# Delaying two stages of a row-tile loop by one tile: the GELU sigmoid and the layernorm backward of a gated-MLP block

## The chip, the cores and the metric

The kernel runs on one core of a Trainium2 chip. The metric is device time in microseconds of one execution. The kernel before takes 1046.89 us (median of 6 runs, 1042.96 to 1053.63); its profiled execution took 1043.44 us, with a span of 1041.7 us from the first to the last instruction.

A core has five engines with instruction streams of their own: PE (matrix multiply, with its weight loads shown as PEld), DVE (vector), ACT (scalar functions), POOL and SP. Each stream is worked through in order. Matrix products land in PSUM, which has 8 banks of 512 float32 values per partition; ACT or DVE bring them from there to SBUF. Transfers to and from HBM are issued by SP, ACT or POOL.

## What is computed

The reference is forward and backward of two pre-layernorm blocks on x of 2048 rows (S) by 512 columns (D), in bfloat16: a linear attention block, then a gated MLP whose gate mixes the rows. Outputs are the result and the gradients of x and of six weights. Cut to what the change touches:

```python
def _B_ref(x, w_in, w_sp, b_sp, w_out):        # F = 1376, Fh = 688
    z = gelu_tanh(x @ w_in)                    # S x F
    z1 = z[..., :Fh]
    z2 = layernorm(z[..., Fh:])
    g = w_sp @ z2 + b_sp                       # mixes rows: S x S times S x Fh
    return (z1 * g) @ w_out

h = x + A(layernorm(x))
out = h + B(layernorm(h))
# and the vjp of out with respect to x and the weights, for a given grad_out
```

The kernel writes tanh-GELU as z * sigmoid(1.5958 * (z + 0.0447 z^3)). Its derivative needs z and the sigmoid s again: dz = (s + z * s * (1 - s) * (a + 3ab z^2)) * dgelu. So forward stores z (tensor `XZ`) and s (tensor `SG`) in HBM and backward loads them.

## The kernel before

It is written in a language whose framework orders each engine's instructions itself: the program gives the operations and the buffer pools, and the framework places the instructions of each engine by their dependences and its own estimates of time, and adds the waits. A pool with `bufs=2` gives two copies of each tile of it; a tile name that is asked for again takes the older copy and waits until all its users are done. There are 16 row tiles (NT) of 128 rows (P), DC = 4 column chunks of D, and 11 chunks of F (the last of 96).

Forward: `hnF` is the normalised h, transposed. The loads of `WspT` are transposing transfers issued from SP.

```python
# psZ: 2 buffers of 3 PSUM banks; xm, sgm: 4 buffers; x2, wt: 2 buffers
for m in range(NT):
    dma_T(WspT[:, m, :], B_w_sp[:, m * P:(m + 1) * P])
...
for m in range(NT):
    psz = psZ.tile(...)
    mm(psz, hnF chunk m, Win)                                        # 12 matmuls
    xm = p2r.tile([P, F], BF16, name="xm")
    nc.scalar.activation(xm[:], psz[:, 0:F], AF.Copy)                # line 474
    dma(XZ_v[:, m, 0:F], xm[:], nc.gpsimd)
    x2 = p2q.tile(...)
    nc.vector.tensor_tensor(out=x2[:], in0=xm[:], in1=xm[:], op=ALU.mult)        # 478
    nc.vector.tensor_scalar(x2[:], x2[:], b_c, 1.0, op0=ALU.mult, op1=ALU.add)   # 480
    wt = p2q.tile(...)
    nc.vector.tensor_tensor(out=wt[:], in0=x2[:], in1=xm[:], op=ALU.mult)        # 483
    sg = p2r.tile([P, F], BF16, name="sgm")
    nc.scalar.activation(sg[:], wt[:], AF.Sigmoid, scale=a_c)        # line 486
    dma(SG_v[:, m, 0:F], sg[:], nc.scalar)
    nc.vector.tensor_tensor(out=zT[:, m, :], in0=xm[:], in1=sg[:], op=ALU.mult)  # 489
ln_stats_all(p2s, lambda m: zT[:, m, Fh:F], ...)                     # bn_stats, line 213
for m in range(NT):
    # normalise zT[:, m, Fh:F] in place                              # line 494
...
for t in range(NT):                                                  # g: 16 x 32 matmuls
    mm(psg, WspT[:, m, t-th chunk], zT[:, m, Fh:])                   # over all m
```

Backward, the stage with the second loop. `pssp` holds 2 banks, `psW` 3, `ps3bt` 2 and `psH` 1: eight in all.

```python
for t in range(NT):                       # gradient of w_sp (out_5), 2 x 12 matmuls per t
    ... psw5 -> w5 (ACT) -> out_5

NJ1 = min(3, DC)
psw0 = psW.tile([P, NJ1, 512], F32, name="psw4")
for m in range(NT):
    # load sm (SG), xm2 (XZ), dzm (DZG)
    # dZT[:, m, :] = (s + z s (1 - s) (a + 3ab z^2)) * dzm    six DVE operations, one on ACT
    for j in range(NJ1):                                             # line 737
        nc.tensor.matmul(psw0[:, j, :], hnT2[:, m, j-th chunk], dZT[:, m, 0:512], ...)
    # 11 transposes of dZT[:, m] into pstZ (line 741), evicted to dzf by ACT
    psd = psH.tile([P, 512], F32, name="psdh")
    mm(psd[:, :], dzf, WinT)                                         # 11 matmuls
    # doutm <- grad_out
    ln_bwd(psd, hnT2[:, m], ..., dhT[:, m, :], resid=doutm)          # lines 223 to 241

# w_in gradient (out_4): jobs (j, gi), 4 column chunks x 3 groups of F, NJ1 jobs per pass
with tc.tile_pool(name="p3bo", bufs=2) as p3bo:
    for pi, job in enumerate([first] + passes):
        if pi > 0:
            psw0 = psW.tile([P, NJ1, 512], F32, name="psw4")         # one buffer
            # 16 x NJ1 matmuls                                       # line 767
        for slot, (j, gi) in enumerate(job):
            w4 = p3bo.tile([P, 512], BF16, name="w4")
            evac_copy(w4, psw0[:, slot])
            dma(out_4[...], w4)
```

After it `oT2` is loaded and `dhT` transposed (line 813) into `dhF`, both where this stage's tiles had lain; 64 matmuls of `oT2` with `dhT` follow (`psw4o`, line 819), and a loop that multiplies `dhF` with `WoT`, copies it on ACT (line 831) and works on it on DVE (lines 834 to 841).

Of the kernel before, what the change touches and what calls it, by code (L numbers as in the profile page):

```python
# [8 lines left out]
BF16 = mybir.dt.bfloat16  # L9
# [4 lines left out]
P = 128  # L14
# [13 lines left out]
def kernel(  # L28
# [74 lines left out]
    def note(eng, ns):  # L103
        busy[eng] += ns
# [354 lines left out]
    with tc.tile_pool(name="p2w", bufs=1) as p2w, \  # L459
            tc.tile_pool(name="p2s", bufs=6) as p2s, \  # L460
            tc.tile_pool(name="psZ", bufs=2, space=bass.MemoryType.PSUM) as psZ, \
            tc.tile_pool(name="ps2t", bufs=1, space=bass.MemoryType.PSUM) as ps2t:
        WspT = p2w.tile([P, NT, S], BF16, name="WspT")
        for m in range(NT):
            dma_T(WspT[:, m, :], B_w_sp[:, m * P:(m + 1) * P])

        with tc.tile_pool(name="p2r", bufs=4) as p2r, tc.tile_pool(name="p2q", bufs=2) as p2q:
            for m in range(NT):
                psz = psZ.tile([P, max(F, D)], F32, name="psZ")
                for (gs, gw) in F_grp:  # L470
                    mm(psz[:, gs:gs + gw],
                       [(hnF[:, j, m * P:(m + 1) * P], Win[:, j, gs:gs + gw]) for j in range(DC)])
                xm = p2r.tile([P, F], BF16, name="xm")
                nc.scalar.activation(xm[:], psz[:, 0:F], AF.Copy)  # L474
                note("act", (172 + F) / 1.2)
                dma(XZ_v[:, m, 0:F], xm[:], nc.gpsimd)
                x2 = p2q.tile([P, F], BF16, name="x2")
                nc.vector.tensor_tensor(out=x2[:], in0=xm[:], in1=xm[:], op=ALU.mult)
                note("dve", (58 + F / 2) / 0.96)
                nc.vector.tensor_scalar(x2[:], x2[:], b_c, 1.0, op0=ALU.mult, op1=ALU.add)  # L480
                note("dve", (58 + F / 4) / 0.96)
                wt = p2q.tile([P, F], BF16, name="wt")
                nc.vector.tensor_tensor(out=wt[:], in0=x2[:], in1=xm[:], op=ALU.mult)
                note("dve", (58 + F / 2) / 0.96)
                sg = p2r.tile([P, F], BF16, name="sgm")
                nc.scalar.activation(sg[:], wt[:], AF.Sigmoid, scale=a_c)  # L486
                note("act", (222 + F) / 1.2)
                dma(SG_v[:, m, 0:F], sg[:], nc.scalar)
                nc.vector.tensor_tensor(out=zT[:, m, :], in0=xm[:], in1=sg[:], op=ALU.mult)
                note("dve", (58 + F / 2) / 0.96)  # L490
        p2R_stack.close()
        ln_stats_all(p2s, lambda m: zT[:, m, Fh:F], Fh, mean3[:], rstd3[:], "3")
        for m in range(NT):
            nc.vector.tensor_scalar(zT[:, m, Fh:F], zT[:, m, Fh:F], mean3[:, m:m + 1], rstd3[:, m:m + 1],  # L494
                                    op0=ALU.subtract, op1=ALU.mult)
            note("dve", (58 + Fh / 4) / 0.96)
        if "zg" in dbg:
            dma(dbg["zg"].rearrange("(m p) f -> p m f", p=P), zT[:], nc.sync)

        gR = gR_stack.enter_context(tc.tile_pool(name="gR", bufs=1, side="right"))  # L500
        GT = gR.tile([P, NT, Fh], BF16, name="GT")
        pre3 = pre3_stack.enter_context(tc.tile_pool(name="pre3", bufs=1, side="right"))
        Wout_n = pre3.tile([P, NFHC, D], BF16, name="Wout_n")
        for k, (ks, kw) in enumerate(Fh_ch):
            dma(Wout_n[:kw, k, :], B_w_out[ks:ks + kw, :], nc.scalar)
        doutT = pre3.tile([P, NT, D], BF16, name="doutT")
        dma(doutT[:], G_v, nc.gpsimd)

        for t in range(NT):
            psg = psZ.tile([P, max(F, D)], F32, name="psZ")  # L510
            for (gs, gw) in Fh_grp:
                mm(psg[:, gs:gs + gw],
                   [(WspT[:, m, t * P:(t + 1) * P], zT[:, m, Fh + gs:Fh + gs + gw]) for m in range(NT)])
            nc.scalar.activation(GT[:, t, :], psg[:, 0:Fh], AF.Identity, bias=bspT[:, t:t + 1])  # L514
            note("act", (172 + Fh) / 1.2)
        if "G" in dbg:
            dma(dbg["G"].rearrange("(m p) f -> p m f", p=P), GT[:], nc.sync)
        uR = uR_stack.enter_context(tc.tile_pool(name="uR", bufs=1, side="right"))
        UT = uR.tile([P, NT, Fh], BF16, name="UT")
        nc.vector.tensor_tensor(out=UT[:], in0=zT[:, :, 0:Fh], in1=GT[:], op=ALU.mult)  # L520
        note("dve", (58 + NT * Fh / 2) / 0.96)
# [138 lines left out]
    with tc.tile_pool(name="p3b", bufs=1) as p3b, \  # L660
# [1 line left out]
            tc.tile_pool(name="pssp", bufs=1, space=bass.MemoryType.PSUM) as pssp, \  # L662
            tc.tile_pool(name="psW", bufs=1, space=bass.MemoryType.PSUM) as psW, \
            tc.tile_pool(name="ps3bt", bufs=1, space=bass.MemoryType.PSUM) as ps3bt, \
            tc.tile_pool(name="psH", bufs=1, space=bass.MemoryType.PSUM) as psH:
        WinT = p3b.tile([P, NFC, D], BF16, name="WinT")
        for k in range(NFF):
            dma_T(WinT[:, k, :], B_w_in[:, k * P:(k + 1) * P])
# [19 lines left out]
        with tc.tile_pool(name="p3sp", bufs=2) as p3sp:  # L688
# [15 lines left out]
                    dma(out_5[t * P:(t + 1) * P, rs0:rs0 + width], w5[:].rearrange("p a b -> p (a b)")[:, 0:width],  # L704
                        nc.sync if t % 2 == 0 else nc.gpsimd)

            NJ1 = min(3, DC)
            cg0s, cg0w = F_grp[0]
            psw0 = psW.tile([P, NJ1, 512], F32, name="psw4")
            with tc.tile_pool(name="p3bg", bufs=2) as p3bg, \  # L710
                    tc.tile_pool(name="p3bd", bufs=2) as p3bd:
                for m in range(NT):
                    sm = p3bg.tile([P, F], BF16, name="sm")
                    dma(sm[:], SG_v[:, m, 0:F], nc.scalar)
                    xm = p3bg.tile([P, F], BF16, name="xm2")
                    dma(xm[:], XZ_v[:, m, 0:F], nc.scalar)
                    dzm = p3bg.tile([P, F], BF16, name="dzm")
                    dma(dzm[:], DZG_v[:, m, 0:F], nc.sync)
                    q1 = p3bg.tile([P, F], BF16, name="q1")
                    nc.vector.tensor_scalar(q1[:], sm[:], -1.0, 1.0, op0=ALU.mult, op1=ALU.add)  # L720
                    note("dve", (58 + F / 4) / 0.96)
                    nc.vector.tensor_tensor(out=q1[:], in0=q1[:], in1=sm[:], op=ALU.mult)
                    note("dve", (58 + F / 2) / 0.96)
                    r0 = p3bg.tile([P, F], BF16, name="r0")
                    nc.scalar.activation(r0[:], xm[:], AF.Square, scale=sq3ab)
                    note("act", (222 + F) / 1.2)
                    nc.vector.scalar_tensor_tensor(out=r0[:], in0=r0[:], scalar=a_c, in1=xm[:],
                                                   op0=ALU.add, op1=ALU.mult)
                    note("dve", (58 + F / 2) / 0.96)
                    nc.vector.tensor_tensor(out=r0[:], in0=r0[:], in1=q1[:], op=ALU.mult)  # L730
                    note("dve", (58 + F / 2) / 0.96)
                    nc.vector.tensor_tensor(out=r0[:], in0=r0[:], in1=sm[:], op=ALU.add)
                    note("dve", (58 + F / 2) / 0.96)
                    nc.vector.tensor_tensor(out=dZT[:, m, :], in0=r0[:], in1=dzm[:], op=ALU.mult)  # L734
                    note("dve", (58 + F / 2) / 0.96)
                    for j in range(NJ1):
                        nc.tensor.matmul(psw0[:, j, :cg0w], hnT2[:, m, j * P:(j + 1) * P], dZT[:, m, cg0s:cg0s + cg0w],  # L737
                                         start=(m == 0), stop=(m == NT - 1))
                    pst = ps3bt.tile([P, NTZ, P], BF16, name="pstZ")
                    for k, (ks, kw) in enumerate(F_ch):  # L740
                        nc.tensor.transpose(pst[:kw, k, :], dZT[:, m, ks:ks + kw], ident[:])
                    dzf = p3bd.tile([P, NFC, P], BF16, name="dzf")
                    if NFF:
                        evac_copy(dzf[:, 0:NFF, :], pst[:, 0:NFF, :], NFF * P / 2, prefer="act")
                    if NFF < NFC:
                        evac_copy(dzf[:LFW, NFF, :], pst[:LFW, NFF, :], P / 2, prefer="act")
                    psd = psH.tile([P, 512], F32, name="psdh")
                    mm(psd[:, :], [(dzf[:kw, k, :], WinT[:kw, k, :]) for k, (ks, kw) in enumerate(F_ch)])
                    doutm = p3bd.tile([P, D], BF16, name="doutm")
                    dma(doutm[:], G_v[:, m, :], nc.sync)  # L750
                    ln_bwd(p3bd, psd[:, :], hnT2[:, m, :], rstd2[:, m:m + 1], D, dhT[:, m, :], "2", resid=doutm[:])
            if "dZ" in dbg:
                dma(dbg["dZ"].rearrange("(m p) f -> p m f", p=P), dZT[:], nc.sync)
            if "dh" in dbg:
# [248 lines left out]
```

## Time and profile before

| | busy us | share of the span |
|---|---|---|
| PE | 777.4 | 75% |
| PEld | 396.8 | 38% |
| DVE | 474.3 | 46% |
| ACT | 362.1 | 35% |
| POOL | 92.6 | 9% |

The profile also has the span in 40 slices of 26 us. Each digit is the busy share of a slice in tenths; PEclk is the clock granted to PE, in tenths:

```profile
PE   0799656546799798257995169999998398459997
DVE  3686864749400230330453089992140057420348
ACT  0881307436211502146111046654430342038122
PEclk9999878867899899789998569999998699659999
```

The GELU loop lies in slices 7 to 10, the second stage in slices 23 to 31. Other views of the same trace are the waits (who waited for whom, total us, times, longest), the timeline (start us, duration us, engine, line, operation, output and inputs, and in brackets the idle time before it with what ended it) and the busy time of each engine in chosen stretches (PE, PEld, DVE, ACT, POOL, each with its number of instructions; then the granted PE clock, the DMA share and GB/s).

### The profile page before, as it was taken

The page shows a single profiled execution, that of the slowest core. Times are in us where ns is not written, and L with a number is a line of the kernel's source. Part 1 is how long each engine was busy: PE and PEld are TensorE (multiplying, and loading weights), DVE is VectorE, ACT ScalarE, POOL GpSimd, SP SyncE. Part 2 cuts the span into 40 slices and gives each one's busy share as a digit, 9 for nine tenths or more (in the row PEclk, how much of TensorE's full clock was granted, in tenths as well). Part 3 has the DMA queues.
Part 4 walks back from the last instruction along what each step waited for, and adds up shares of the span by engine and source line. Part 5 has one row for each costly group of instructions (what it writes and reads, how often), then busy time and mean ns, then how long its engine had stood idle before and what let it go on. Part 6 is the DMA issues. An engine that isn't in the chain of part 4 may idle for free.

```text
span 1041.7 us, 12513 instructions
## 1 busy us (share of the span) xinstructions
PE 777.4 (75%) x4809; PEld 396.8 (38%) x4809; DVE 474.3 (46%) x1003; ACT 362.1 (35%) x558; POOL 92.6 (9%) x159
## 2 busy tenths in 40 slices
PE   0799656546799798257995169999998398459997
PEld 0436424212466433144653023433444245135443
DVE  3686864749400230330453089992140057420348
ACT  0881307436211502146111046654430342038122
POOL 1030212101000010223001000000000000000000
PEclk9999878867899899789998569999998699659999
DMA  5333244999300740936102966752110902422111
GB/s 176 127 114 139 81 142 160 217 260 275 119 1 1 135 136 32 360 110 174 42 35 83 335 201 222 226 178 79 68 41 24 244 28 82 162 81 82 46 46 51
DMA packets 114411, 133.26 MB, mean 128 GB/s; under 512 B 64560, under 2 KB 87808, under 8 KB 114352
## 3 DMA queue, kind: packets, MB, share of 16 engines
q1 hardware_dynamic: 78064, 48.15, 17.2%
q0 software_dynamic: 14272, 50.74, 14.2%
q10 hardware_dynamic: 22016, 33.58, 10.1%
q8 instruction: 37, 0.61, 0.2%
q14 instruction: 22, 0.18, 0.1%
HBM read 61.72 MB, written 56.12 MB: 113 GB/s over the span
## 4 chain that ended last, share of the span: by engine, by line
issue 19%; PE 19%; DMA 9%; DVE 7%; ACT 2%; SPq 2%; POOL 2%; POOLq 0%; ACTq 0%; DVEq 0%
PE psd L115 6%; PE psw4o L115 4%; SPq L110 2%; PE psw4o L819 1%; DMA emkF_7290<-EMKT 1%; DVE dkF L914 1%; DMA Wsp_n<-in_B_w_sp_dram 1%; DMA oT_6485<-OO 1%; DMA xnT_7449<-XN 1%; POOL out_dram L107 1%; DMA DGF<-trg 1%; DVE dnumT L841 1%; DMA pkF_7344<-PKT 1%; DMA WinT<-in_B_w_in_dram 1%; PE psdh L115 1%
## 5 line engine op out<-in xcount | busy, mean ns | idle before, releaser
L115 PE MATMUL psZ<-zT,WspT 128*128 128x176 bf16 (+1 forms) x512 | 76.8, 313 | 13.9 <-DVE zT L494 13.9
L115 PE MATMUL psd<-dGT,Wsp_n 128*128 128x176 bf16 (+1 forms) x512 | 74.8, 309 | 2.4 <-ACT trg L99 2.4
L115 PE MATMUL psZ<-Win,hnF 128*128 128x512 bf16 (+1 forms) x192 | 50.0, 416 | 32.3 <-ACT xm L474 32.3
L115 PEld LDWEIGHTS <-dGF_4761 128*128 128x128 bf16 (+1 forms) x384 | 34.8, 98 | 78.2 <-issue 50.4
L115 PEld LDWEIGHTS <-WspT 128*128 128x128 bf16 x512 | 44.8, 99 | 46.1 <-DMA doutT<-in_grad_out_dram 14.3
L115 PEld LDWEIGHTS <-Wsp_n 128*128 128x128 bf16 x512 | 44.5, 98 | 32.6 <-issue 2.2
L115 PE MATMUL psdh<-WinT,dzf 128*128 128x512 bf16 (+1 forms) x176 | 42.9, 381 | 0.2
L115 PEld LDWEIGHTS <-hnF 128*128 128x128 bf16 x192 | 20.6, 110 | 55.6 <-issue 43.9
L520 DVE TENSOR_TENSOR UT<-zT,GT 128x11008 bf16<-128x11008 bf16 x1 | 5.9, 5891 | 72.3 <-ACT GT L514 72.3
L834 DVE TENSOR_TENSOR prodo<-dom,oT_6485 128x512 bf16<-128x512 bf16 x16 | 6.6, 414 | 69.4 <-DMA WqkvT<-in_A_wqkv_dram 56.5
L115 PE MATMUL psu<-WoutT,doutF 128*128 128x512 bf16 (+1 forms) x128 | 20.6, 325 | 21.5 <-ACT dum L595 18.4
L514 ACT ACTIVATE GT<-psZ,bspT 128x688 bf16<-128x688 f32 x16 | 13.4, 835 | 65.2 <-PE psZ L115 65.2
L486 ACT ACTIVATE sgm<-wt 128x1376 bf16<-128x1376 bf16 x16 | 21.5, 1349 | 23.3 <-DMA WspT<-in_B_w_sp_dram 12.1
L597 DVE CUSTOM_DVE_ANT_0 dGT<-dum,zT 128x688 bf16<-128x688 bf16 x16 | 13.9, 872 | 30.8 <-ACT dum L595 30.7
L99 ACT ACTIVATE trg<-pstG 128x1280 bf16<-128x1280 bf16 (+1 forms) x32 | 22.9, 800 | 12.0 <-DMA out_dram<-dbrow 9.0
L737 PE MATMUL psw_5327<-dZT,hnT 128*128 128x512 bf16 x48 | 14.1, 396 | 16.9 <-DVE dZT L734 16.9
L474 ACT ACTIVATE xm<-psZ 128x1376 bf16<-128x1376 f32 x16 | 20.6, 1321 | 17.0 <-DMA WspT<-in_B_w_sp_dram 12.8
L115 PEld LDWEIGHTS <-xnT_7449 128*128 128x128 bf16 x192 | 18.2, 98 | 21.5 <-DMA xnT_7449<-XN 1.9
L564 PE MATMUL psw<-doutT,UT 128*128 128x512 bf16 x96 | 24.3, 384 | 0.8 <-DVE h2row L554 0.8
L767 PEld LDWEIGHTS <-hnT 128*128 128x128 bf16 x144 | 15.4, 108 | 22.4 <-issue 9.2
L282 PE MATMUL pst_217<-ident,xnT 128*128 128x128 bf16 x8 | 1.2, 308 | 30.5 <-DVE xnT L272 30.4
L115 PEld LDWEIGHTS <-dzf 128*128 128x128 bf16 (+1 forms) x176 | 15.1, 98 | 21.9 <-issue 5.2
(1512 smaller groups left out, 1637.8 us busy)
## 6 DMA issues: line engine op xcount, KB each, us to landing
XZ<-xm POOLq DMA_DIRECT2D x16, 344.0 KB, 5.0
SG<-sgm ACTq DMA_DIRECT2D x16, 344.0 KB, 4.7
sm<-SG ACTq DMA_DIRECT2D x16, 344.0 KB, 3.6
dzm<-DZG SPq DMA_DIRECT2D x16, 344.0 KB, 4.2
Wsp_n<-in_B_w_sp_dram SPq DMA_DIRECT2D x8, 512.0 KB, 10.9
Wsp_n<-in_B_w_sp_dram POOLq DMA_DIRECT2D x8, 512.0 KB, 14.1
DGF<-trg POOLq DMA_DIRECT2D x8, 320.0 KB, 3.2
Z2F<-trg POOLq DMA_DIRECT2D x8, 320.0 KB, 3.2
```

What stands on the lines that cost most here:

```text
L99: return nc.scalar.activation(dst, src, AF.Copy)
L107: return eng.dma_start(out_ap, in_ap)
L110: return nc.sync.dma_start_transpose(out_ap, in_ap)
L115: nc.tensor.matmul(ps, l, r, start=(i == 0), stop=(i == n - 1))
L474: nc.scalar.activation(xm[:], psz[:, 0:F], AF.Copy)
L486: nc.scalar.activation(sg[:], wt[:], AF.Sigmoid, scale=a_c)
L514: nc.scalar.activation(GT[:, t, :], psg[:, 0:Fh], AF.Identity, bias=bspT[:, t:t + 1])
L564: nc.tensor.matmul(psw[:kw, k, :], UT[:, m, ks:ks + kw], doutT[:, m, :], start=(m == 0), stop=(m == NT - 1))
L597: nc.vector.tensor_tensor_reduce(out=dGT[:, m, :], in0=dum[:], in1=zT[:, m, 0:Fh], scale=1.0, scalar=0.0, op0=ALU.mult, op1=ALU.add, accum ...
L737: nc.tensor.matmul(psw0[:, j, :cg0w], hnT2[:, m, j * P:(j + 1) * P], dZT[:, m, cg0s:cg0s + cg0w], start=(m == 0), stop=(m == NT - 1))
L767: nc.tensor.matmul(psw0[:, slot, :gw], hnT2[:, m, j * P:(j + 1) * P], dZT[:, m, gs:gs + gw], start=(m == 0), stop=(m == NT - 1))
L819: nc.tensor.matmul(psw[:, jd, :], oT2[:, m, jd * P:(jd + 1) * P], dhT[:, m, :], start=(m == 0), stop=(m == NT - 1))
```

## The change

Two loops are skewed by one row tile, so that in the text of iteration m the tail of tile m - 1 stands behind the head of tile m. In the GELU loop the tail is the sigmoid, its store and the product; in the backward loop it is the layernorm backward. The aim is that no engine waits for a result of the same tile that another engine has only just begun. For this, pools grow: `p2q` (x2, wt) from 2 to 3 buffers, `p3bd` from 2 to 3, and `psH` from one PSUM bank to two, so that the product of tile m may be written while tile m - 1 is read. The eight banks are full, so `psW` gives one up: NJ1 goes from 3 to 2, and the 12 column jobs of out_4 go in six passes of two where they went in four of three.

```diff
-        with tc.tile_pool(name="p2r", bufs=4) as p2r, tc.tile_pool(name="p2q", bufs=2) as p2q:
-            for m in range(NT):
+        with tc.tile_pool(name="p2r", bufs=4) as p2r, tc.tile_pool(name="p2q", bufs=3) as p2q:
+            xm_l = [None] * NT
+            wt_l = [None] * NT
+            for m in range(NT + 1):
+                if m < NT:
                     ... matmuls, xm, XZ store, x2, wt as before
+                    xm_l[m] = xm
+                    wt_l[m] = wt
+                if m >= 1:
+                    mp = m - 1
+                    sg = p2r.tile([P, F], BF16, name="sgm")
+                    nc.scalar.activation(sg[:], wt_l[mp][:], AF.Sigmoid, scale=a_c)
+                    dma(SG_v[:, mp, 0:F], sg[:], nc.scalar)
+                    nc.vector.tensor_tensor(out=zT[:, mp, :], in0=xm_l[mp][:], in1=sg[:], op=ALU.mult)
...
-            tc.tile_pool(name="psH", bufs=1, space=bass.MemoryType.PSUM) as psH:
+            tc.tile_pool(name="psH", bufs=2, space=bass.MemoryType.PSUM) as psH:
...
-            NJ1 = min(3, DC)
+            NJ1 = min(2, DC)
...
-                    tc.tile_pool(name="p3bd", bufs=2) as p3bd:
-                for m in range(NT):
+                    tc.tile_pool(name="p3bd", bufs=3) as p3bd:
+                for m in range(NT + 1):
+                    if m < NT:
                         ... loads, dZ, line 737 products, transposes, dzf, psd as before
+                        psd_l[m] = psd
+                    if m >= 1:
+                        mp = m - 1
+                        doutm = p3bd.tile([P, D], BF16, name="doutm")
+                        dma(doutm[:], G_v[:, mp, :], nc.sync)
+                        ln_bwd(p3bd, psd_l[mp][:, :], hnT2[:, mp, :], rstd2[:, mp:mp + 1], D, dhT[:, mp, :], "2",
+                               resid=doutm[:])
```

## Prediction

> **What bounds the kernel now.** I read the busy table and the slices first, to see whether one engine bounds the whole run. None does: PE is busy 75% of the span and DVE 46%, with stages that change hands. So I read the two stages the change touches by themselves, and the stretch after the second one.
>
> Stage A is the GELU forward loop (lines 467 to 494 of the kernel, about 175 to 267 us). The waits of that window, total us, times, longest:
>
> ```profile
> PE psZ L115 <- ACT xm L474: 32.3, 6, 14.0
> ...
> ACT xm L474 <- DMA WspT<-in_B_w_sp_dram: 12.8, 2, 10.0
> ...
> ACT sgm L486 <- DMA WspT<-in_B_w_sp_dram: 12.1, 1, 12.1
> ACT sgm L486 <- DVE wt L483: 11.2, 8, 3.4
> ```
>
> The wait that the pipelining aims at is the last line: ACT's sigmoid waits for DVE's cubic, 11.2 us in 8 times. But the two lines above it are larger, 12.8 + 12.1 = 24.9 us, and there ACT waits for a *transfer* that its arithmetic does not need. The built program explains this. Every transfer issued from SP or ACT counts on one of eight completion counters, handed out in turn, and a new transfer may be issued only when the previous user of its counter has landed. The store of each sigmoid tile is issued from ACT's own in-order stream, so where its counter was last used by a transposing load of `WspT` (16 of them, issued back to back from 186.89 us), ACT stands still with all that follows. In the timeline:
>
> ```profile
> 197.60 13.05 ACTq L107 DMA_DIRECT2D SG<-sgm  x2
> ...
> 210.97 1.35 ACT L486 ACTIVATE sgm<-wt 128x1376 bf16<-128x1376 bf16 x1 [12.14 <-DMA WspT<-in_B_w_sp_dram]
> ...
> 232.61 2.53 ACT L474 ACTIVATE xm<-psZ 128x1376 bf16<-128x1376 f32 x2 [9.99 <-DMA WspT<-in_B_w_sp_dram]
> ```
>
> By the built order the store of tile 4 waits for transpose 3, tile 5 for transpose 5, tile 7 for transpose 10. Their releases in the trace (210.6, 215.9, 232.2 us) give (232.2 - 215.9)/5 = 3.26 us per transpose. Stage A is therefore paced by the transposes up to 232 us. After that it is paced by DVE, which is busy 15.86 of the 17 us from 250 to 267. The stage ends on DVE's last statistics and the normalisation, for which the next 76.8 us of PE work wait (PE idle 13.9 us before line 494's result).
>
> Stage B is the dZ and layernorm-backward loop together with the out_5 products (590 to 757 us), then the passes that finish out_4 (to 808), then the load of `oT2`. Busy us by engine in each stretch (PE, PEld, DVE, ACT, POOL):
>
> ```profile
> 640.00:700.00 60.00, 59.92 (x292) 23.72 (x290) 57.87 (x87) 34.48 (x55) 3.78 (x7) 1.00 0.68 219
> 700.00:757.00 57.00, 56.97 (x277) 22.51 (x276) 13.56 (x32) 25.01 (x48) 3.89 (x8) 1.00 0.19 70
> 757.00:772.00 15.00, 14.22 (x89) 7.02 (x88) 7.37 (x18) 6.50 (x13) 0.43 (x1) 1.00 0.17 54
> 772.00:808.00 36.00, 28.80 (x144) 14.70 (x142) 2.46 (x6) 4.58 (x10) 1.61 (x3) 0.86 0.06 21
> ```
>
> From 610 to 757 PE has no gap at all: the scheduler already fills every wait of the row-tile chain with out_5 products. So the loop that is to be pipelined has nothing to give. From 757 to 808 there are gaps of 0.8 + 7.2 us, and the timeline shows where:
>
> ```profile
> 781.75 0.60 ACT L99 ACTIVATE w_6347<-psw_6292 128x512 bf16<-128x512 f32 x1 [1.89 <-DMA out_dram<-w_6341]
> ...
> 796.66 0.46 ACT L99 ACTIVATE w_6405<-psw_6350 128x352 bf16<-128x352 f32 x1 [2.00 <-DMA out_dram<-w_6399]
> ...
> 814.57 0.46 ACT L99 ACTIVATE w_6463<-psw_6408 128x352 bf16<-128x352 f32 x1 [6.42 <-DMA out_dram<-w_6457]
> ```
>
> A pass evicts three banks through two `w4` buffers, so the third eviction waits until the first one's store has landed, and PE waits for it (2.76 and 3.69 us before the next pass, 0.65 us at the first).
>
> **What the Trainium skill says.** "DMA: Bandwidth & Descriptors", section "Issuing engines are not separate DMA queues": transfers from all issuing engines share the same 16 DMA engines. The trace agrees: stage A's 344 KB stores take 4.7 and 5.0 us (medians) to land while the transposes run, and loads of that size in stage B 3.6 and 4.2. "Perfetto Trace Analysis", section "Summary: the profiler window per engine type": the bar of an SP or ACT transfer shows the lock wait and the descriptor work, not the movement. So the 13.05 us bar above is not data moving. "Perfetto Trace Analysis", section "Optimization Strategy": a gap that repeats can mean too few buffers. The repeated gap at the out_4 passes fits this. "PSUM — Partial Sum Buffer", section "The four PSUM rules": a matmul output fits one bank of 8. This is why the second `psH` bank has to be taken from `psw4` (2 + 3 + 2 + 1 before, 2 + 2 + 2 + 2 after).
>
> **The change, part by part.**
>
> *1. Stage A order.* No arithmetic is added or removed: 16 tiles of one PSUM copy (1.31 us) and one sigmoid (1.35) on ACT, of 0.79 + 0.43 + 0.79 (cubic) and 0.79 + 0.94 + 0.2 (product, statistics) on DVE, taken as start-to-start distances in the timeline: 2.0 + 1.9 = 3.9 us of DVE per tile. ACT becomes strictly sigmoid m, copy m+2, store m. The stores then draw other counters. In the built order tile 3 waits for transpose 1, tile 4 for 3, 5 for 5, 6 for 7, 7 for 9, 8 for none, 9 for 11, 10 for 12, 12 for 13. So the lockstep with the transposes remains, but its last binding wait is transpose 9 instead of 10, and the copy is one tile ahead when it ends. Before, at 232.2: sigmoids up to 7 done, cubics up to 8; DVE starts at 233.96 with 7 x 2.0 + 8 x 1.9 = 29.2 us of work and is done at 264.95, 31.0 later. After: release at 232.2 - 3.26 = 229.0, sigmoid 8 done at 230.4, cubics up to 9 done; DVE has 6 x 2.0 + 8 x 1.9 = 27.2 us, times 31.0/29.2 = 28.9, done at 259.3. **Gain 5.6 us, taken as 5.5.** Tiles 9 to 15 should not be held again: transposes 11 to 15 land from 235 to 249 and those stores come 4 us apart from about 235.
>
> *2. Stage B order, psH doubled, p3bd at 3 buffers.* PE's built order holds the same matmuls: before each tile's transposes stand as many or one more out_5 groups. The first dZ needs the same loads behind the same transposes, so the start (PE idle 16.9 us to 609) stays. **Gain 0.**
>
> *3. psw4 at two banks.* 12 column jobs of 16 matmuls stay 12; in the loop 32 matmuls stand instead of 48, but the second pass now begins inside the loop, and after the last `psdh` group 128 matmuls remain against 127. Boundaries that PE feels: before 0.65 + 2.76 + 3.69 = 7.1 us. After, with two evictions and two buffers, no eviction waits for a store: 0.2 + 0.49 + 0.60 = 1.3 us for 512 columns, 0.2 + 0.36 + 0.46 = 1.0 for 352. One boundary lies beside 16 transposes of `dhT` (1.05 us), the others cost 1.3 and 1.0. About 2.7. **Gain 4.4 us.**
>
> *4. Behind the last pass.* Before: last matmul at 807.25; third eviction at 814.57; its store lands at 819.46; then `oT2`, whose space was `w4`'s, is asked for at 820.73 and PE starts on it at 831.76: 24.5 us after the last matmul. After: both evictions end about 1.1 us after it, the stores land 4 to 6.4 us later (4.13 and 6.40 before), `oT2` needs 11 to 13: 17 to 20, say 18.5. Gain 6. Part of it is given back. PE's built order now puts the `oT2` products (64, 14 us) ahead of 16 of the `dhT` transposes (1.2 us) and of the first two tiles of line 831, which DVE before did while PE worked (2 x 1.63 = 3.3 us); about 0.9 comes back because ACT no longer evicts `psw4o` first. **Gain 6 - 1.2 - 3.3 + 0.9 = 2.4 us.**
>
> Sum 5.5 + 0 + 4.4 + 2.4 = 12.3 us: 1046.9 - 12.3 = **1034.6, taken as 1035 us**. The last stages follow by data and should move as a block.
>
> **Rivals.**
> *a. The transposes take all of part 1.* If they land later than before, because stores now run beside them where ACT's standstill left them alone, the release at transpose 9 slips and part 1 gives nothing: about 1040. For it: the DMA share is above 1.0 in those windows. Against it: their issue on SP is one unbroken bar of 59 us, before and during the standstill.
> *b. The pipelining works as meant.* ACT's 11.2 us on the cubic and the standstill both go: stage A becomes DVE-bound from 185 us, 16 x 3.9 = 63 us, ending near 250: about 1023. Against it: tiles 3 to 7 still wait on transposes 1 to 9.
> *c. DVE or ACT becomes the bound in stage B.* DVE is busy 57.87 of 60 us from 640 to 700; an order that feeds PE's transposes later would open gaps, some 5 to 10 us, about 1042. Against it: the built order gives DVE one out_5 group (3.06 us) more of time.
> *d. The five passes cost more than three,* if the evictions were not hidden: at most 2 x 1.3 us more, about 1037.
>
> **Range and chances.** Part 1 may give 0 to 12, part 3 2 to 5, part 4 -2 to 6, and the six times of before spread by 10.7 us, their median being worth some +-3. The range is 1025 to 1043. Two per cent is 20.9 us, which needs rival b with all else: 0.09. Slower by as much needs a new wait of 33 us over my sum: 0.02.
>
> **What the profile after would show.** Part 1: ACT still waiting for `WspT`, in several shorter waits, and line 494's normalisation starting about 5.5 us earlier. Part 2: PE without gaps between the first dZ and the last `psdh`, no shorter than before. Part 3: no eviction waiting for an out_4 store; gaps of 1.0 to 1.3 us between passes. Part 4: `oT2` about 18.5 us behind the last pass, with no line 834 product during line 819. I am wrong if the transposes pace differently, or if the clock granted to PE (0.86 in the passes) moves.

## The result, and the profile after

The changed kernel takes 1038.24 us (median of 20 runs, 1033.07 to 1047.51) against 1049.01 us (median of 40, 1041.53 to 1062.56) of the kernel before in the same series: a ratio of 0.9914, 95% interval 0.989 to 0.9938. The profiled span went from 1041.7 to 1033.0 us. The predicted time was 1035 us with a range of 1025 to 1043. The time is inside it, but the parts are not what the sum said.

To see where the time went I compared when the same piece of work stands in both profiles. "Lead" is how much earlier the changed kernel is there.

| event (us) | before | after | lead |
|---|---|---|---|
| first copy of stage A on ACT | 174.79 | 176.81 | -2.0 |
| last GELU product ends | 263.74 | 253.43 | 10.3 |
| normalisation behind stage A starts | 266.24 | 257.62 | 8.6 |
| first dZ product on PE | 609.02 | 600.75 | 8.3 |
| last `psdh` product ends | 772.05 | 763.48 | 8.6 |
| last out_4 product ends | 807.25 | 790.72 | 16.5 |
| first `oT2` product | 831.76 | 810.92 | 20.8 |
| last `dnumT` row tile on DVE ends | 870.61 | 855.60 | 15.0 |
| first `dq` product | 880.14 | 865.13 | 15.0 |
| last `dq` product ends | 892.17 | 881.55 | 10.6 |
| end of the span | 1041.7 | 1033.0 | 8.7 |

The lead is won twice, in stage A and in the out_4 passes, and a good part of it is lost again behind the passes. The code ahead of stage A is the same in both kernels; its 2.0 us are variation from run to run.

**Stage A.** The waits of 175 to 267 us in the profile after (total us, times, longest):

```profile
PE psZ L115 <- ACT xm L477: 20.1, 9, 3.6
PE psZ L115 <- DVE zT L501: 14.7, 1, 14.7
DVE zT L496 <- ACT sgm L493: 12.7, 6, 3.6
ACT sgm L493 <- DMA WspT<-in_B_w_sp_dram: 9.1, 2, 5.2
ACT sgm L493 <- DVE wt L486: 8.9, 6, 3.5
...
ACT L217 <- DMA SG<-sgm: 3.3, 1, 3.3
ACT sgm L493 <- DVE lnst_2310 L213: 3.3, 1, 3.3
ACT sgm L493 <- DVE lnst_2330 L213: 3.1, 1, 3.1
```

ACT still waits for the loads of `WspT`, in shorter waits, as foretold. But the names in this list mislead. Where a store in ACT's stream is held and the next sigmoid waits behind it, the view may name a DVE instruction that was done long before. In the timeline of one such wait:

```profile
205.45 0.85 DVE L486 TENSOR_TENSOR wt<-x_2056,xm 128x1376 bf16<-128x1376 bf16 x1
214.16 0.33 ACTq L107 DMA_DIRECT2D SG<-sgm  x1
214.59 1.35 ACT L493 ACTIVATE sgm<-wt 128x1376 bf16<-128x1376 bf16 x1 [3.53 <-DVE wt L486]
```

The cubic was done at 206.30; what ended the wait was the store ahead of it. By the trace's landing times seven stores (tiles 3 to 7, 9 and 10) left 0.08 us after the landing of the transposes 1, 3, 5, 7, 9, 11 and 12, just those of the built order. The waits behind these seven come to 23.2 us, with 5.2 the longest. In the kernel before they were 24.9 us in three waits, with 12.1 the longest, so their sum hardly changed. The wait at which the pipelining aims, for the cubic, fell from 11.2 us to 5.4, once the 3.53 above is taken from the 8.9. What changed most is that DVE has something to do while ACT stands. Busy us of PE, PEld, DVE, ACT and POOL in the same 64 us, first the kernel before, then the changed one:

```profile
177.00:241.00 64.00, 34.13 (x152) 15.46 (x151) 38.16 (x67) 31.85 (x31) 9.81 (x17) 0.76 1.08 247
```

```profile
177.00:241.00 64.00, 43.77 (x194) 19.72 (x193) 46.23 (x80) 39.06 (x39) 11.48 (x20) 0.84 1.07 274
```

DVE, the third busy figure, does 8.1 us more work in the same time, at the same DMA share (1.08 and 1.07).

**Stage B and the passes.** Four stretches of the profile after; they are those of the prediction, shifted by the lead:

```profile
632.00:692.00 60.00, 59.72 (x291) 23.69 (x290) 57.31 (x87) 34.17 (x56) 3.78 (x7) 1.00 0.66 209
692.00:748.00 56.00, 55.84 (x273) 22.16 (x272) 11.60 (x29) 24.48 (x48) 4.32 (x8) 1.00 0.22 78
748.00:763.00 15.00, 14.56 (x91) 7.16 (x90) 8.07 (x20) 7.04 (x14) 0.54 (x1) 1.00 0.10 27
763.00:791.00 28.00, 25.22 (x147) 13.53 (x145) 2.46 (x6) 3.87 (x9) 1.62 (x3) 1.00 0.09 31
```

PE is as full in the loop as it was before. The passes are 28 us long instead of 36 and, in the last but two column, they run at a granted clock of 1.00 instead of 0.86. In the timeline no eviction waits for a store, and PE waits 0.33, 1.22 and 0.95 us for the eviction ahead of it (0.31 at the pass before these):

```profile
771.61 7.07 PE L780 MATMUL psw_6351<-dZT,hnT 128*128 128x512 bf16 x32 [0.33 <-ACT w_6348 L99]
...
779.90 4.93 PE L780 MATMUL psw_6390<-dZT,hnT 128*128 128x352 bf16 x32 [1.22 <-ACT w_6387 L99]
...
785.79 4.93 PE L780 MATMUL psw_6429<-dZT,hnT 128*128 128x352 bf16 x32 [0.95 <-ACT w_6426 L99]
```

The clock of the kernel before fell right behind its two long gaps:

```profile
782.30:785.70 3.40, 3.30 (x9) 1.28 (x9) 0.00 (x0) 0.05 (x1) 0.00 (x0) 0.51 0.12 39
797.20:802.80 5.60, 5.60 (x20) 2.91 (x20) 0.00 (x0) 0.00 (x0) 0.00 (x0) 0.50 0.07 19
```

**Behind the passes.** The two chains of the timeline that set the end of the stage, after:

```profile
800.11 1.19 POOL L107 DMA_DIRECT2D oT_6487<-OO  x1 [7.65 <-DMA out_dram<-w_6462]
810.92 1.46 PE L832 MATMUL psw4o<-dhT,oT_6487 128*128 128x512 bf16 x3 [6.53 <-DMA oT_6487<-OO]
...
827.50 2.06 ACT L99 ACTIVATE w_6682<-psw4o 128x512 bf16<-128x512 f32 x4 [11.71 <-PE psw4o L832]
829.42 0.63 ACT L844 ACTIVATE dom<-ps_6689 128x512 bf16<-128x512 f32 x1
...
830.08 0.42 DVE L847 TENSOR_TENSOR prodo<-dom,oT_6487 128x512 bf16<-128x512 bf16 x1 [63.20 <-ACT dom L844]
```

`oT2` is asked for 9.4 us after the last pass, when the stores of `w4` have landed, and used 20.2 us after it (24.5 before). Then DVE starts on its row tiles only behind the products and behind ACT's eviction of `psw4o`, with all 16 tiles to do where it had 14 left before.

**The dq stage.** Here PE's clock differs. The first line is of the kernel before, the second of the changed one:

```profile
883.00:893.00 10.00, 9.51 (x40) 3.00 (x39) 8.98 (x14) 0.00 (x0) 0.00 (x0) 1.00 0.01 2
```

```profile
868.00:883.00 15.00, 14.84 (x40) 3.65 (x39) 9.49 (x14) 0.00 (x0) 0.00 (x0) 0.53 0.01 1
```

The same 40 matmuls take 14.84 us instead of 9.51, at a clock of 0.53 instead of 1.00, with no transfer beside them. This eats 4.4 us of the lead.

### The profile page after: what moved, and what is told of

Same layout as the page of the kernel before. It is cut to its first block, busy times and chain, and to the rows that moved or that the text cites. A ratio compares the mean times of both kernels' runs of the same rounds, so it can differ in the third digit from the quotient of the medians.

```text
span 1033.0 us, 12518 instructions
## 1 busy us (share of the span) xinstructions
PE 782.8 (76%) x4809; PEld 398.2 (39%) x4809; DVE 472.2 (46%) x1003; ACT 361.7 (35%) x558; POOL 92.3 (9%) x159
## 5 line engine op out<-in xcount | busy, mean ns | idle before, releaser
L521 ACT ACTIVATE GT<-psZ,bspT 128x688 bf16<-128x688 f32 x16 | 13.4, 835 | 65.2 <-PE psZ L115 65.2
L604 DVE CUSTOM_DVE_ANT_0 dGT<-dum,zT 128x688 bf16<-128x688 bf16 x16 | 13.9, 872 | 30.7 <-ACT dum L602 30.5
L115 PEld LDWEIGHTS <-dzf 128*128 128x128 bf16 (+1 forms) x176 | 15.2, 98 | 22.3 <-issue 5.0
L115 PEld LDWEIGHTS <-doutF 128*128 128x128 bf16 x128 | 11.7, 101 | 30.6 <-issue 23.6
L99 ACT ACTIVATE dzf<-pstZ 128x1280 bf16<-128x1280 bf16 (+1 forms) x32 | 22.4, 758 | 0.2 <-PE pstZ L750 0.2
## 6 DMA issues: line engine op xcount, KB each, us to landing
Wsp_n<-in_B_w_sp_dram POOLq DMA_DIRECT2D x8, 512.0 KB, 13.6
```

Source lines behind the costliest of these rows:

```text
L99: return nc.scalar.activation(dst, src, AF.Copy)
L115: nc.tensor.matmul(ps, l, r, start=(i == 0), stop=(i == n - 1))
L604: nc.vector.tensor_tensor_reduce(out=dGT[:, m, :], in0=dum[:], in1=zT[:, m, 0:Fh], scale=1.0, scalar=0.0, op0=ALU.mult, op1=ALU.add, accum ...
```

## The experiments

Every comparison is with runs of the kernel before on the same chip in the same series; their median was 1051.9 to 1053.0 us in all of these, so the ratios are to be compared, not the times. All ratios at a glance:

| run | ratio to before | 95% interval |
|---|---|---|
| stage A order alone | 0.9924 | 0.9894 to 0.9954 |
| stage B edit alone | 0.9949 | 0.9924 to 0.9973 |
| stage B banks and buffers, loop not skewed | 0.9947 | 0.9923 to 0.9971 |
| before with three `w4` buffers | 0.9967 | 0.9941 to 0.9993 |
| before, sigmoid stores from GpSimd | 1.0343 | 1.0292 to 1.0394 |
| changed, sigmoid stores from GpSimd | 1.0131 | 1.0079 to 1.0183 |
| before, `WspT` loaded plainly | 0.9832 | 0.9788 to 0.9875 |
| changed, `WspT` loaded plainly | 0.9768 | 0.9725 to 0.9812 |
| changed, `Wout_n` from SP | 0.9845 | 0.9804 to 0.9886 |
| new order A, stores on SP, three `w4` | 0.9901 | 0.9865 to 0.9937 |
| old order A, stores on SP, three `w4` | 0.9899 | 0.9851 to 0.9947 |
| changed kernel again | 0.9899 | 0.9847 to 0.9951 |

### The two halves apart

Stage A alone takes the GELU loop of the changed kernel and leaves stage B as it was; stage B alone is the reverse.

> The kernel before with only the new order of stage A (the GELU loop with its sigmoid one tile behind); stage B as before. My theory: the 10.6 us by which the changed kernel shortens stage A come from this order alone, so the normalisation behind stage A starts 8 to 11 us earlier than in the kernel before (266.2 us there), stage B takes as long as before, and the time falls by 8 to 10 us. Rival (the gain comes from the stage B edit and the rest is drift): the time stays within 3 us of before.

> The kernel before with only the stage B edit (loop skewed by one row tile, psH at two banks, psw4 at two banks, p3bd at three buffers); stage A as before. My theory: the out_4 passes have 2.8 us of gaps instead of 7.1, the oT2 products start 20 us behind the last pass instead of 24.5, then the part behind gives back about 6 because DVE has two more row tiles to do after those products: net -2 to -4 us of the whole. Rival (the pipelining is what helps): the first-dZ to last-psdh stretch, 163 us before, becomes shorter by more than 2 us, and the time falls by 8 or more.

The ratios say 0.8% and 0.5%, about 8.0 and 5.4 us of 1053. Both are gains of their own, so the rival of the first run falls by its time. In its profile the last GELU product ended at 254.96 us, 8.8 earlier than before, but the normalisation started only at 264.22:

```profile
258.78 0.33 ACTq L107 DMA_DIRECT2D SG<-sgm  x1
259.13 3.13 ACTq L107 DMA_DIRECT2D Wout_n<-in_B_w_out_dram  x5
262.30 1.28 ACT L217 ACT_TABLE_LOAD   x1 [8.36 <-issue]
```

The square root that the normalisation needs stands in ACT's stream behind the last sigmoid store and five loads of `Wout_n`; in this execution the last transpose was issued so late (SP's bar of the 16 ended at 251.6 us, in the changed kernel's profile at 244.5) that the store left only at 258.78. So the expectation of 8 to 11 us at the normalisation failed in this profile (2.0 us, or 3.9 counted from stage A's first copy), for a reason that belongs to the same lockstep: this store left 0.08 us after the last transpose had landed.

In the stage B run the first dZ stands at 607.96 and the last `psdh` ends at 770.58: 162.6 us against 163.0 before. The rival (a shorter loop) falls. The passes then take 27.2 us instead of 35.2, and the stretch from the last pass to the last `dnumT` 64.3 instead of 63.4. The time fell by a little more than the 2 to 4 us expected. Added up, the halves give 1.3% where the whole gives 0.9 to 1.0%; the intervals are too wide to call that a loss.

### Skew or banks

Only buffer sizes against the kernel before:

```
-            tc.tile_pool(name="psH", bufs=1, ...) as psH:
+            tc.tile_pool(name="psH", bufs=2, ...) as psH:
-            NJ1 = min(3, DC)
+            NJ1 = min(2, DC)
-                    tc.tile_pool(name="p3bd", bufs=2) as p3bd:
+                    tc.tile_pool(name="p3bd", bufs=3) as p3bd:
```

> As the stage B edit (psH two banks, psw4 two banks, p3bd three buffers), but the loop keeps its order of before: each tile's layernorm backward right behind its own psdh product. My theory: the skew itself does nothing, so this takes the same time as the full stage B edit within 2 us, with gaps of 1 to 1.3 us between the out_4 passes. Rival: the skew is worth something, and this is over 3 us slower than the full stage B edit.

Ratio 0.9947 against 0.9949 of the full edit: the skew of stage B is worth nothing that can be measured. From the first dZ to the last `dnumT` this run takes 255.5 us, the full edit 254.2, the kernel before 261.6. The gain belongs to the bank split; the third `p3bd` buffer was not run apart, but the gaps that closed are those of the passes, where that pool is no longer in use. (Skew with one `psH` bank wasn't tried: a tile's product would need the bank that the tile before still holds.)

### A third buffer instead

```
-            with tc.tile_pool(name="p3bo", bufs=2) as p3bo:
+            with tc.tile_pool(name="p3bo", bufs=3) as p3bo:
```

> The kernel before with a third w4 buffer for the out_4 evictions, nothing else. My theory: the third eviction of a pass no longer waits for a store, so the gaps of 2.76 and 3.69 us before the passes fall to about 1.2 each and the eviction behind the last pass ends some 5 us earlier, and oT2 is asked for earlier by as much: time 4 to 8 us less, as the DVE does two tiles beside PE as before. Rival (the gap is PSUM eviction itself, not the store): gaps stay above 2 us and the time stays the same within 2 us.

This is the other way to the same end: three banks, three buffers. Its timeline in the passes:

```profile
781.18 9.45 PE L767 MATMUL psw<-dZT,hnT 128*128 128x512 bf16 x47 [0.77 <-ACT w L99]
790.72 1.44 ACT L99 ACTIVATE w<-psw 128x512 bf16<-128x512 f32 x3 [9.59 <-PE psw L767]
792.21 7.32 PE L767 MATMUL psw<-dZT,hnT 128*128 128x352 bf16 x48 [1.58 <-ACT w L99]
```

The gaps are 0.77 and 1.58 us instead of 2.76 and 3.69, so the store was the cause, and the rival falls. The passes take 26.5 us, even less than the changed kernel's 27.2: a shorter gap is not all of it. The 48 matmuls of 352 columns take 7.32 us here and 10.07 before, the same work at a clock of 1.00 and of 0.72. The clock of the passes sorts the profiles: in the kernel before and the three others with its passes (stage A alone, stores from GpSimd, plain loads), PE ran at half the clock for 3 to 6 us in all four right behind the gap of 3.7 us, and in three of four behind that of 2.8; in the other nine whose profile is read, with gaps of at most 1.6 us, it never did inside the passes. The Trainium skill, "Perfetto Trace Analysis", section "Optimization Strategy", reads a repeating gap as a possible sign of too few buffers; this run agrees, and with the gaps the low clock went too.

The whole gives only 3.5 us (0.9967), because the stretch behind the passes is longer: 68.5 us from the last pass to the last `dnumT`, against 63.4 before. The last eviction did end over 5 us earlier, but `oT2` was asked for only 2 us earlier (11.5 us behind the last pass, 13.5 before), since the last store took 8.2 us to land. Here too the `oT2` products came ahead of all 16 DVE tiles, although nothing else of the program was changed: PE's built order has them first. My expectation of two tiles beside PE failed, and why the order came out so wasn't looked into.

### Taking the stores off ACT

```
-                dma(SG_v[:, m, 0:F], sg[:], nc.scalar)
+                dma(SG_v[:, m, 0:F], sg[:], nc.gpsimd)
```

> The kernel before with one word changed in stage A: the store of each sigmoid tile is issued from GpSimd instead of from ACT's own stream. My theory (ACT stands still because its stores wait for the transposing loads of WspT, not because sigmoid and cubic alternate): the waits of ACT on WspT, 24.9 us before, go, the last GELU product ends near 250 us instead of 263.7, and the time falls by 8 to 13 us, as much as or more than the new order gives, although the loop keeps the old order. Rival (the alternation of sigmoid and cubic is the bound): stage A ends within 3 us of before. A second rival: the stores then wait in GpSimd's stream, the transposes get slower beside them, and the product behind stage A waits for the last transpose instead.

> The changed kernel with the sigmoid stores issued from GpSimd. My theory: ACT is free of the transposes in the new order too; stage A is DVE-bound from 185 us (16 x 3.9 us), the last GELU product ends at 248 to 251 us instead of 253.4, and the normalisation can follow at once: 3 to 6 us less than the changed kernel. Against the same store placement in the old order the new order is worth 0 to 4 us. Rival (the new order is needed): it is over 6 us faster than the old order with the same stores.

Both became slower, by 3.4% and 1.3%. Of the second rival of the first run one part holds, the slower transposes. The transposing loads, changed kernel with stores from GpSimd:

```profile
L110 SPq DMA_TRANSPOSE WspT<-in_B_w_sp_dram x16: 1953/4110/16115, 186.9 to 275.2; - x16
...
DMA to landing us min/median/max: 4.5/7.1/30.6
```

The last is issued at 275.2 us (240.4 in the changed kernel) and one took 30.6 us to land (10.6 at most in the changed kernel, 14.8 in the kernel before). And ACT was not free of them after all. Its wait in the same profile:

```profile
ACT L217 <- DMA WspT<-in_B_w_sp_dram: 30.6, 1, 30.6
```

The loads of `Wout_n`, issued from ACT ahead of the square root, count on the counters of the transposes too. In the old order they stand even ahead of the last four sigmoids, which waited 22.4 and 13.4 us behind them; the last GELU product ended there at 279.98 us, 16.2 later than before, where 250 was expected.

In the new order the last product ended at 246.11 us, 7.3 earlier than in the changed kernel, and no wait on `WspT` was left inside the loop. But this is not the gain that the theory meant. With the stores elsewhere the framework also placed the layernorm statistics of 14 of the 16 tiles behind the last product (3 in the changed kernel). At some 0.9 us a tile that is about 10 us of DVE work moved out of the loop (an estimate). So the runs show that the stores hold ACT, and that moving them to this queue moves the wait; what the loop gains without them they don't show.

### Without the transposition

The loads of `WspT` are made plain, of the same size; this leaves the transposition out, and the product behind stage A uses the matrix as it lies.

```
-            dma_T(WspT[:, m, :], B_w_sp[:, m * P:(m + 1) * P])
+            dma(WspT[:, m, :], B_w_sp[m * P:(m + 1) * P, :], nc.sync)
```

> The kernel before with the 16 loads of WspT as plain loads of the same 512 KB each, without the transposition (so the product behind stage A uses the untransposed matrix: this leaves the transposition out). My theory: the plain loads land faster than the transposing ones, 1.4 to 2.5 us each by the loads of before's other stages, so ACT's stores stop waiting by about 220 us, and stage A ends near 250 to 254 us in the old order. Rival (ACT's stalls come from the arithmetic order): it still ends at 260 us or later.

> The changed kernel with the same plain loads of WspT in place of the transposing ones (this leaves the transposition out). My theory: with the transposes gone both orders are DVE-bound in stage A, so this differs from the old order with plain loads by at most 2 us in the end of stage A, and in the whole time by what the stage B edit gives, 4 to 6 us. Rival (the pipelining works by itself): the end of stage A comes over 4 us earlier than in the old order with plain loads, and the time is 9 or more us less.

Counted from stage A's first copy, the normalisation starts after 74.0 us in the old order and after 68.7 in the new; with the transposing loads it was 91.5 and 80.8. So the transposition costs 17.4 us of stage A in the old order and 12.1 in the new. The old order's last product ended at 248.51 us and its normalisation began at 250.76, so the theory of the first run held and its rival falls. But my expectation for the pair failed: I wrote that without them the two orders would be within 2 us, and they are 5.4 us apart. DVE's busy time shows it, old order and then new:

```profile
177.00:241.00 64.00, 45.59 (x206) 20.91 (x204) 53.99 (x97) 43.61 (x41) 12.62 (x21) 0.84 0.82 315
```

```profile
177.00:241.00 64.00, 41.09 (x203) 19.49 (x200) 57.75 (x103) 46.66 (x43) 13.00 (x22) 0.86 0.85 331
```

DVE works 57.75 of 64 us in the new order, 53.99 in the old. In the old order it waits 4.8 us for ACT's copies (0.7 in the new). So the new order ended stage A earlier here too, as the rival said. That it does so by itself isn't shown, for the plain loads still hold ACT's stores: one store of the old order left 0.08 us after a load of `WspT` had landed (ACT waited 3.9 us, and DVE stood for 2.5 of its 4.8 us right behind that), six stores of the new order did, and there DVE went on. In the whole time the two runs are 0.64% apart, with intervals of 0.4% on either side, so the time alone does not tell 5 from 9 us.

### Where else ACT can be freed

```
-            dma(Wout_n[:kw, k, :], B_w_out[ks:ks + kw, :], nc.scalar)
+            dma(Wout_n[:kw, k, :], B_w_out[ks:ks + kw, :], nc.sync)
```

> The changed kernel with the six loads of Wout_n issued from SP instead of ACT. In the changed kernel ACT issues them, and waits for their completion counters, ahead of the square root of the statistics: 252.8 to 255.7 us, and 3.1 us late again in the run with the new order of stage A alone. My theory: the normalisation starts 1.5 to 3.5 us earlier than in the changed kernel, counted from its last GELU product (4.2 us there), and the time is 1 to 3 us less; the last sigmoid store can still hold ACT. Rival (statistics on DVE end last): no change of that distance. On the dq stage: if its low clock follows from the new order of the stages before it, it shows here too.

> The changed kernel itself once more, for a second profile of it and as the companion of the run with Wout_n on SP, which came out at a ratio of 0.9845 although its profile shows the normalisation only 1 us nearer to the last GELU product. If the Wout_n placement is worth what that ratio says, this stays near 0.991, and about 7 us above it. Rival (the two are the same kernel within what a set of runs can tell): a ratio of 0.984 to 0.989. Low clock in the dq stage: if it belongs to this kernel's order, the stage takes 15 to 17 us again; if it is chance, 11 to 12 us in this profile.

With `Wout_n` on SP the distance from the last GELU product to the normalisation was 3.2 us; in the two profiles of the changed kernel it was 4.2 and 3.8. That is 0.6 to 1.0 us, less than the 1.5 to 3.5 expected. The last sigmoid store still holds ACT (2.0 us on `WspT` ahead of the table load), but the square root then waits 0.3 us more for DVE's last statistics. So these end the distance now, as the rival had it for the whole. The ratio of 0.9845 is the lowest of all versions that compute the reference. The changed kernel on the same chip came to 0.9899; the intervals overlap (0.9804 to 0.9886 and 0.9847 to 0.9951), so it is not shown that this version beats it.

The other attempt put the store and one transposing load in turn into SP's stream, so that ACT issues nothing in the loop, with `Wout_n` on SP and three `w4` buffers in the old stage B; once with the new order of stage A, once with the old:

```
                 dma_T(WspT[:, m, :], B_w_sp[:, m * P:(m + 1) * P])   # now inside the loop
-                dma(SG_v[:, m, 0:F], sg[:], nc.scalar)
+                dma(SG_v[:, m, 0:F], sg[:], nc.sync)
```

> New order of stage A, with each sigmoid store issued from SP and one transposing load of WspT issued between two of them (so ACT issues and awaits no transfer in the loop), Wout_n from SP too; stage B as before but with three w4 buffers. My theory: ACT no longer waits for transfers, stage A is DVE-bound from 185 us and its last GELU product ends at 242 to 248 us, the last transpose lands by 255, and with the third w4 buffer the time is 15 to 20 us less than before, 1029 to 1035. Rival (the transposes become the bound): spread over the loop they land after 260 us, the product behind stage A waits for them, and the time is 1040 or more.

> As the run with the sigmoid stores on SP between the transposing loads, Wout_n on SP and three w4 buffers, but stage A in its old order. Theory after the runs with plain loads (there the new order gave 5.7 us by the start of the normalisation although no transpose was near): about half of the gain of stage A is the order itself, so here the normalisation starts 4 to 7 us later than with the new order, and the time is 4 to 7 us more. Rival (the first theory: all of it is the lockstep with the transposes): within 2 us of the new order.

Ratios 0.9901 and 0.9899: no better than the changed kernel, and alike. The theory of 15 to 20 us falls. In the profile of the new order the wait has changed its name:

```profile
ACT sgm L493 <- DMA SG<-sgm: 24.7, 11, 4.9
...
253.00:265.30 12.30, 0.00 (x0) 0.00 (x0) 12.23 (x42) 0.11 (x2) 1.18 (x1) 0.50 1.08 256
...
265.27 0.31 ACT L217 ACTIVATE rstd<-lnmv,eps_t 128x16 f32<-128x16 f32 x1 [12.19 <-DVE lnmv L215]
```

The first line is of the waits, the second of the busy times, the third of the timeline. The stores now queue behind the transposes on SP, and ACT waits for one of the four `sgm` buffers. The end of the stage is set by DVE: here too the statistics of 14 of the 16 tiles stand behind the last product (252.69 us), and DVE works 12.23 of the next 12.30 us on them while PE has nothing to do. The program with the old order has 11 of 16 there. The profile of the old order fell in a disturbed execution, and no time is read from it, here or below. So neither run shows stage A with ACT freed and the rest as it was, and why the two orders take the same time here stays open.

### The clock in the dq stage

Length of the stage from the first to the end of the last `dq` product in the profiles:

| profile | dq stage, us |
|---|---|
| before; stage A alone; three `w4` buffers | 12.0; 10.7; 10.7 |
| changed; changed again | 16.4; 15.1 |
| stage B edit; banks without skew | 15.2; 13.6 |
| before and changed with plain `WspT` | 17.6; 16.4 |
| before and changed with sigmoid stores from GpSimd | 16.4; 18.0 |
| `Wout_n` on SP; stores on SP, new order | 15.0; 12.7 |

The low clock begins inside the stage in the ten lower profiles, and only in the PE pause behind it in the three upper ones. It returned in the second profile of the changed kernel. Yet it isn't tied to the stage B edit, since the kernel before has it too with plain loads and with stores from GpSimd, nor to a moment of the span (it begins between 857 and 915 us). What sets it stays open.

## Why the prediction was right, and where its steps were wrong

**Part 1, 5.5 us.** The profile gives 8.6 us at the normalisation. The place was right: the stores stay in lockstep with the transposes, which set the stage. (The 13.05 us bar that the prediction shows as such a store is two bars of 0.33 and 0.37 us, at 197.60 and 210.27, which the view merges; ACT stood between them.) The count of DVE's work behind the release was right as well: when sigmoid 8 was done, cubics up to 9 and eight products were done, as put, and DVE ended 28.3 us later where 28.9 was put. The term that was mis-sized is the release of tile 7's store. It was put at 229.0, from a pace of the transposes of 3.26 us taken as fixed. It came at 225.91, transposes 5 to 9 having landed at a pace of 2.94. In the second profile of the changed kernel it came at 229.67, so this pace is not fixed from one execution to the next, and 225.91 was luck in part. "Tiles 9 to 15 should not be held again" failed too: tiles 9 and 10 cost ACT 3.1 and 1.5 us, but DVE had other work for most of that. The second profile of the changed kernel has the normalisation 81.8 us behind the first copy, the first 80.8; four profiles in the old order have 87.6 to 92.4, 90.4 on average. That is a gain of 8.6 to 9.6. The single run with stage A alone has 87.6, so one profile can be 7 us off.

**Part 2, nothing.** Right: 163.0 us from the first dZ to the last `psdh` before, 162.7 after, and the loop without skew gives the same ratio.

**Part 3, 4.4 us.** The gaps went from 7.1 to 0.31 + 0.33 + 1.22 + 0.95 = 2.8 us: a gain of 4.3, as worked out. But the stretch from the last `psdh` to the last out_4 product became 8.0 us shorter, and only 3.9 of that are gaps that lie in it. The rest is clock that the gaps had cost: PE worked 8.9 us at half the clock behind them, which is worth about 4.4, and none afterwards. The sum had no term for it; the prediction only named the clock as a thing that might move.

**Part 4, 2.4 us.** The sign was wrong: 63.4 us from the last pass to the last `dnumT` before, 64.9 after, a loss of 1.5. `oT2` came after 20.2 us, not 18.5, because the two last stores of `w4` took 6.9 and 7.3 us to land, and their landing was put at 4 to 6.4. From there on the stage takes 44.7 us instead of 38.9, a loss of 5.8 where 1.2 + 3.3 - 0.9 = 3.6 was put. The 0.9 never came back: ACT evicted `psw4o` (2.06 us) ahead of the first `dom`, as before.

**"The last stages ... should move as a block"** is the step that failed outright: 4.4 us lost in the dq stage and 1.9 behind it, with a clock that nobody had changed on purpose.

**The rivals.** Rival a falls: the stage gained more than the prediction said. Rival b was refused because of the transposes, rightly for this kernel, although the wait for the cubic did halve; with them gone the changed kernel runs at 0.9768, and 0.9768 of 1049 is 1025 us, about the 1023 that b had. Rivals c and d fall: PE is full from 632 to 763 us and the passes are shorter. The sum of 12.3 us came near the 8.7 of the profiles and the 9.0 that the ratio of 0.9914 makes of 1049 partly by luck: the errors of parts 1 and 3 (+3.1 and +3.6) make up for two thirds of those of part 4 and of the last stages (-3.9 and -6.3).

## What to carry to other kernels

Before you reorder arithmetic, look at what the in-order stream of the engine carries besides arithmetic: a store issued from ACT waited here for transposing loads of another queue, and no order of the sigmoids removed that. When an eviction waits for a store, count the buffers against the evictions per pass; one more buffer, or one bank less, closed the gap and kept the clock. When a store moves to another queue, look at what else the framework then places elsewhere: here the statistics went behind the loop, so an earlier end of the loop alone said little about the stage. And follow an early result to the end: what came 20.8 us earlier was worth 8.7 at the end of the span.

## What the hardware showed that was not expected

- On a busy PE a gap of 3.7 us was followed by 3 to 6 us of PE work at half the granted clock in four of four profiles, one of 2.8 us in three of four, gaps up to 1.6 us in none of nine. In the kernel before the two gaps cost about 4 us on top of themselves.
- Moving 16 stores of 344 KB from ACT's to GpSimd's queue went with a slowest transposing load beside them of 30.6 us to land where it had been 10.6 (changed kernel), and of 30.5 where it had been 14.8 (kernel before), in one profile each.
- A run's time tends to go with its mean granted clock: of the changed kernel's runs, those with 0.872 took 1043 to 1045 us, those with 0.887 to 0.890 1033.5 to 1036.6. It is no rule, for two with 0.879 took 1033.1 and 1044.3, and which of the two moves the other isn't shown.
